# Layer 2 of two units of each pair by seven products summed in PSUM, with the groups ordered by a list scheduler

## The chip, the core and the metric

The kernel runs on one core of a Trainium2 chip. The metric is the device time of the whole program in microseconds (us), the median of three runs. Five engines work in parallel, each through its own queue in order: TensorE (PE in the profile, its weight loads PEld), VectorE (DVE), ScalarE (ACT), GpSimd (POOL) and SyncE (SP, which here only issues DMAs). PE writes to PSUM, which has eight banks of 128 x 512 fp32; the other operands lie in SBUF.

## The reference

A gated recurrence over 2 sequences of 6080 positions and 256 channels gives `h`, and a feed-forward layer with 2048 hidden columns follows:

```
f = lower_bound + (1 - lower_bound) * sigmoid(f_logit);  i = 1 - f
h[t] = f[t] * h[t-1] + i[t] * x[t]          # h starts at 0 in each sequence
a = h @ w_in                                # (12160, 256) @ (256, 2048), layer 1
g = a if a >= 1;  0 if a <= -1;  (a + 1)**2 / 4 between
out = g @ w_out                             # (12160, 2048) @ (2048, 256), layer 2
```

## The kernel before

The 12160 positions are cut into 24 tiles (all of 512 columns but one of 384). The hidden columns are cut into 8 units of 256 (`u`), each of two blocks of 128. Every product is done at nearly fp32 precision: each factor is split into a high and a low part (`xhi`/`xlo`, `ghi`/`glo`, `wi_hi`/`wi_lo`, `wo_hi`/`wo_lo`), and one product of a 128x128 weight block with 128x512 data is three matmuls (high*high, low*high, high*low). The low part of data costs one subtraction, the high part one cast.

**Stages.** The first four tiles, and all work on the weights, run in a first stage whose order is written out by hand (`ORDER`). From then on the 20 remaining tiles go in 10 pairs of neighbours (`pairs`), and each pair goes through the 8 units: 80 groups `g`, eight to a pair. In a group, layer 1 of a pair and a unit is a 2x2 block product (two column halves of the weight against two input halves of two tiles, eight block products), done by Strassen's scheme in Winograd's form with seven products `p1` to `p7` that are summed in PSUM (`pe1`, L988, with the table `SEVEN`, L981). The sums on the data side (`t1` to `t4`) are made in SBUF, and the intermediate sums by copies and additions between PSUM banks: `fork` (L999, ACT) copies bank Y into a new bank Q, `snap` (L994, ACT) copies Z to SBUF, `add_z` and `add_v` (L1004, L1007, DVE) add it to Y. At the end four banks Q, Z, V and Y hold the four blocks of `a`.

Each block then goes through a chain of five operations: `s_clip` (L1021, DVE, to [-1, 1]), `s_sq` (L1027, ACT, square of (c+1)/2), `s_max` (L1031, DVE, maximum with the bank, after which the bank is free), `s_hi_` (L1036, ACT, cast to `ghi`) and `s_lo_` (L1039, POOL, subtraction to `glo`).

**Layer 2** of a group (`fill_mm` and `triples`, L588) is eight products, each three matmuls, into four banks that belong to the pair (2 tiles x 2 output halves, `po`) for all its eight groups. They lag one group behind layer 1, and stand between its products. So a group is 7 + 8 = 15 products, 45 matmuls. At the end of a pair, `finish` (L654) copies the four banks out (three on ACT, one on DVE) and SP stores them. PSUM is full: four banks for the pair, four for the group, and a bank of the next group is one that the group before has given up.

**Order.** For the groups it is a table of times by hand: every operation has an offset from the group's start, `zt(g)` = 10.2 us times g (`at_time`, L956; `chain`, L1074), and all are emitted sorted by that time. The preparation of the next pair (`prepare`, L1125: loads, gate, recurrence `scan` on DVE, sums `t_sum` L915 and splits `f_hi`, `f_lo`) has places in the same table. Pools: three tiles of two blocks each for `g`, `ghi` and `glo` (`gp`, L213), two output tiles `o` (`op`).

Of the kernel before, what the change touches and what calls it, by code (L numbers as in the profile page):

```python
# [159 lines left out]

@with_exitstack
def gated_scan_then_ffn_kernel(
# [8 lines left out]

# [34 lines left out]
    KEPT = 5  # L206
    assert KD == 2 and KF == 16 and (len(tiles) - NC) % 2 == 0
# [5 lines left out]
    gp = ctx.enter_context(tc.tile_pool(name="gp", bufs=3))  # L213
# [305 lines left out]
    def plain_o(t, u, j, d):  # L519
        n = tiles[t][1]  # L520
        if (t, d) not in po:
            po[t, d] = bank()
        first = (t, d) not in started
        started.add((t, d))
        nc.tensor.matmul(  # L525
            out=po[t, d][:, :n], lhsT=vals[2 + 2 * u][:, j, d * P : (d + 1) * P], rhs=gg[t, u][:, j, :n],
            start=first, stop=False,
        )

    def clip(t, u, j):  # L530
        n = tiles[t][1]
        if (t, u) not in gg:
            gg[t, u] = gp.tile([P, 2, NMAX], F32, tag="g", name="g")
        nc.vector.tensor_scalar(
            out=gg[t, u][:, j, :n], in0=acc[t, u, j][:, :n], scalar1=-1.0, scalar2=1.0,
            op0=ALU.max, op1=ALU.min,
        )
# [3 lines left out]
    def clip_act(t, u, j):  # L541

        n = tiles[t][1]
        if (t, u) not in gg:
            gg[t, u] = gp.tile([P, 2, NMAX], F32, tag="g", name="g")
        c = gg[t, u][:, j, :n]
# [3 lines left out]
    def square(t, u, j):  # L550
        c = gg[t, u][:, j, : tiles[t][1]]
# [5 lines left out]
    def top(t, u, j):  # L557
        n = tiles[t][1]
        c = gg[t, u][:, j, :n]
# [8 lines left out]
    def g_hi(t, u, js=JA):  # L568
        n = tiles[t][1]
        if (t, u) not in ghi:  # L570
            ghi[t, u] = gp.tile([P, 2, NMAX], F32R, tag="ghi", name="ghi")
        s = slice(js[0], js[-1] + 1)
        nc.scalar.copy(out=ghi[t, u][:, s, :n], in_=gg[t, u][:, s, :n])

    def g_lo(t, u, js, eng):
        n = tiles[t][1]
        if (t, u) not in glo:
            glo[t, u] = gp.tile([P, 2, NMAX], F32R, tag="glo", name="glo")
        s = slice(js[0], js[-1] + 1)
        eng.tensor_tensor(  # L580
            out=glo[t, u][:, s, :n], in0=gg[t, u][:, s, :n], in1=ghi[t, u][:, s, :n],
            op=ALU.subtract,
        )

    def triple(t, d, u, i, a, b, first, last):
        triples(t, [d], u, i, a, b, first, last)

    def triples(t, ds, u, i, a, b, first, last, parts=range(3)):  # L588

        n = tiles[t][1]  # L590
        for q in parts:
            for d in ds:
# [5 lines left out]
                    start=not begun, stop=(last and q == 2),  # L598
                )

    def mm_o(t, u, js=JA, ds=range(KD), parts=range(3)):
        n = tiles[t][1]
        for j in js:
            for d in ds:
# [3 lines left out]
                t, ds, u, j, ghi[t, u][:, j, :n], glo[t, u][:, j, :n] if parts[-1] == 2 else None,  # L608
# [74 lines left out]
    with tc.manual_schedule():  # L683
# [156 lines left out]
        for kind, t, u, j in pe:  # L840
# [5 lines left out]
            if kind == "H":  # L846
# [20 lines left out]
                if "O" + i not in plain:  # L867
# [8 lines left out]
                    add("U" + i, "ACT", act(z), deps, g_hi, t, u, [j])  # L876
                    add("L" + i, "DVE|POOL", two(z), ["U" + i], on, g_lo, t, u, [j])
# [76 lines left out]
        ev = []  # L954

        def at_time(when, f, *args):  # L956
            ev.append((when, len(ev), f, args))

        TG = 10.2

        def zt(g):

            return g * TG

        def product(dst, p, u, wname, xname, start):
            if wname[0] == "a":
                i, k = int(wname[1]) - 1, int(wname[2]) - 1
                wh, wl = wi_hi[:, u, k, i], wi_lo[:, u, k, i]
            else:
                q = (int(wname[1]) - 1) * P  # L970
                wh, wl = (s[u // 2][:, u % 2, q : q + P] for s in (s_hi, s_lo))
            h, l = xhi[p, xname], xlo[p, xname]
            for q, (w, r) in enumerate([(wh, h), (wl, h), (wh, l)]):
                nc.tensor.matmul(  # L974
                    out=dst, lhsT=w, rhs=r, start=(start and q == 0), stop=(q == 2),
                    skip_group_check=True,
                )

        B = {}
        snaps = {}  # L980
        SEVEN = (  # L981
# [4 lines left out]
        )  # L986

        def pe1(g, name, role, w, x, start):  # L988
            p, u = divmod(g, NU)
            if (g, role) not in B:  # L990
                B[g, role] = bank()
            product(B[g, role], p, u, w, x, start)

        def snap(g):  # L994
            s = op.tile([P, NMAX], F32, tag="snap", name="snap", bufs=1)
            snaps[g] = s
            nc.scalar.copy(out=s, in_=B[g, "Z"])
# [3 lines left out]

# [9 lines left out]

        blocks = [("Q", 0, 0), ("Z", 1, 0), ("V", 1, 1), ("Y", 0, 1)]

        def gtile(d, g, b, dt, tag):
            if (g, b // 2) not in d:
# [226 lines left out]
```

## Time and profile before

| | |
|---|---|
| time, median of 3 runs (lowest, highest) | 1000.63 us (1000.56, 1000.72) |
| profiled execution, first to last instruction (span) | 999.2 us |
| median time less that span | 1.4 us |
| PE busy, of the span | 991.8 us, 99% |
| DVE, ACT, POOL busy | 741.7, 706.8, 639.7 us |
| first layer 1 product of the pairs starts | 173.5 us |
| granted TensorE clock, mean | 0.999 of full speed |

The profile is one execution of its own; of its time the trace gives the span, and the 1.4 us between it and the median of the timed runs lie outside the first and the last instruction. Busy time of PE counts a matmul from its start to the modelled end of its pipeline, so neighbours overlap: one lasts 0.39 us, but the next starts 0.23 us later.

### The profile page before, as it was taken

The page shows a single profiled execution, that of the slowest core. Times are in us where ns is not written, and L with a number is a line of the kernel's source. Part 1 is how long each engine was busy: PE and PEld are TensorE (multiplying, and loading weights), DVE is VectorE, ACT ScalarE, POOL GpSimd, SP SyncE. Part 2 cuts the span into 40 slices and gives each one's busy share as a digit, 9 for nine tenths or more (in the row PEclk, how much of TensorE's full clock was granted, in tenths as well). Part 3 has the DMA queues.
Part 4 walks back from the last instruction along what each step waited for, and adds up shares of the span by engine and source line. Part 5 has one row for each costly group of instructions (what it writes and reads, how often), then busy time and mean ns, then how long its engine had stood idle before and what let it go on. Part 6 is the DMA issues. An engine that isn't in the chain of part 4 may idle for free.

```text
span 999.2 us, 12745 instructions
## 1 busy us (share of the span) xinstructions
PE 991.8 (99%) x4374; PEld 816.2 (82%) x4374; DVE 741.7 (74%) x1129; ACT 706.8 (71%) x1230; POOL 639.7 (64%) x506
## 2 busy tenths in 40 slices
PE   8999999999999999999999999999999999999998
PEld 3888888888888888888888888888888888888886
DVE  8998998676677678677667668667767767776665
ACT  8988897766775775776676676677577667667555
POOL 1233326567767776876867777777687587777454
PEclk9999999999999999999999999999999999999999
DMA  9221020200200120030020020002002002001001
GB/s 346 85 69 59 22 100 1 85 21 1 106 22 1 48 80 1 0 106 22 1 106 22 0 106 22 1 26 97 5 1 105 22 1 85 1 1 43 0 1 43
DMA packets 17057, 46.56 MB, mean 47 GB/s; under 512 B 1888, under 2 KB 2912, under 8 KB 16992
## 3 DMA queue, kind: packets, MB, share of 16 engines
q1 hardware_dynamic: 16848, 45.62, 12.8%
q8 instruction: 34, 0.56, 0.2%
q14 instruction: 31, 0.25, 0.1%
q10 hardware_dynamic: 144, 0.13, 0.0%
HBM read 33.29 MB, written 12.45 MB: 46 GB/s over the span
## 4 chain that ended last, share of the span: by engine, by line
PE 98%; DVE 1%; DMA 0%; issue 0%; SPq 0%; DVEq 0%
PE bank L596 51%; PE bank L974 38%; PE bank L506 7%; PE bank L525 1%; DMA x<-in_fx 0%; PE bank L517 0%; DVE h L471 0%; DVE x L454 0%; DVE kept L339 0%; DVE kept L323 0%; DVE kept L344 0%; DVE g L562 0%; DVE kept L314 0%; DVE ea L274 0%; DVE o L630 0%
## 5 line engine op out<-in xcount | busy, mean ns | idle before, releaser
L1040 POOL TENSOR_TENSOR glo<-g,ghi 128x512 fp32r<-128x512 f32 x320 | 410.9, 1295 | 236.8 <-ACT ghi L1037 196.6
L1029 ACT ACTIVATE g<-g 128x512 f32<-128x512 f32 x320 | 200.8, 633 | 134.7 <-DVE g L1022 126.9
L1034 DVE TENSOR_TENSOR g<-g,bank 128x512 f32<-128x512 f32 x320 | 219.4, 686 | 80.0 <-ACT g L1029 65.3
L596 PE MATMUL bank<-ghi,wo_hi 128*128 128x512 f32 x759 | 259.0, 388 | 0.0
L596 PE MATMUL bank<-ghi,wo_lo 128*128 128x512 f32 x759 | 258.8, 387 | 0.0
L596 PE MATMUL bank<-glo,wo_hi 128*128 128x512 f32 x759 | 258.7, 387 | 0.0
L1037 ACT CAST ghi<-g 128x512 fp32r<-128x512 f32 x320 | 191.6, 626 | 70.3 <-DVE g L1034 68.5
L1022 DVE TENSOR_SCALAR g<-bank 128x512 f32<-128x512 f32 x320 | 213.8, 689 | 0.1
L596 PEld LDWEIGHTS bank<-ghi,wo_lo 128*128 128x128 f32 x759 | 142.2, 188 | 28.9 <-POOL wo_lo L353 0.3
L596 PEld LDWEIGHTS bank<-ghi,wo_hi 128*128 128x128 f32 x759 | 142.3, 188 | 28.8
L596 PEld LDWEIGHTS bank<-glo,wo_hi 128*128 128x128 f32 x759 | 142.3, 188 | 28.7
L1005 DVE TENSOR_TENSOR bank<-bank,snap 128x512 f32<-128x512 f32 x80 | 56.0, 700 | 111.5 <-ACT ghi L1037 109.4
L974 PE MATMUL bank<-xhi,s_hi 128*128 128x512 f32 x320 | 124.5, 389 | 0.0
L974 PE MATMUL bank<-xhi,s_lo 128*128 128x512 f32 x320 | 124.5, 389 | 0.0
L974 PE MATMUL bank<-xlo,s_hi 128*128 128x512 f32 x320 | 124.5, 389 | 0.0
L974 PE MATMUL bank<-xhi,wi_hi 128*128 128x512 f32 x240 | 93.4, 389 | 0.0
L974 PE MATMUL bank<-xhi,wi_lo 128*128 128x512 f32 x240 | 93.4, 389 | 0.0
L974 PE MATMUL bank<-xlo,wi_hi 128*128 128x512 f32 x240 | 93.4, 389 | 0.0
L1009 DVE TENSOR_TENSOR bank<-bank,snap 128x512 f32<-128x512 f32 x80 | 56.0, 700 | 43.5 <-PE bank L974 43.5
L1002 ACT COPY bank<-bank 128x512 f32<-128x512 f32 x80 | 45.6, 570 | 49.4 <-PE bank L974 49.4
L974 PEld LDWEIGHTS bank<-xlo,s_hi 128*128 128x128 f32 x320 | 60.1, 188 | 12.5
L974 PEld LDWEIGHTS bank<-xhi,s_lo 128*128 128x128 f32 x320 | 60.1, 188 | 12.5
(93 smaller groups left out, 1181.2 us busy)
## 6 DMA issues: line engine op xcount, KB each, us to landing
out_dram<-o SPq DMA_DIRECT2D x45, 256.0 KB, 2.1
f<-in_fx SPq DMA_DIRECT2D x22, 512.0 KB, 4.0
x<-in_fx SPq DMA_DIRECT2D x22, 512.0 KB, 4.3
raw<-in_w_out SPq DMA_DIRECT2D x8, 512.0 KB, 4.3
raw<-in_w_in SPq DMA_DIRECT2D x7, 512.0 KB, 5.6
raw<-in_w_in SPq DMA_DIRECT2D x2, 256.0 KB, 3.5
x<-in_fx SPq DMA_DIRECT2D x2, 256.0 KB, 4.1
f<-in_fx SPq DMA_DIRECT2D x2, 192.0 KB, 4.6
```

What stands on the lines that cost most here:

```text
L506: nc.tensor.matmul(out=acc[t, u, j][:, :n], lhsT=(wi_lo if q == 1 else wi_hi)[:, u, k, j], rhs=(xlo if q == 2 else xhi)[t, k][:, :n], star ...
L525: nc.tensor.matmul(out=po[t, d][:, :n], lhsT=vals[2 + 2 * u][:, j, d * P : (d + 1) * P], rhs=gg[t, u][:, j, :n], start=first, stop=False,)
L596: nc.tensor.matmul(out=po[t, d][:, :n], lhsT=w, rhs=b if q == 2 else a, start=not begun, stop=(last and q == 2),)
L974: nc.tensor.matmul(out=dst, lhsT=w, rhs=r, start=(start and q == 0), stop=(q == 2), skip_group_check=True,)
L1002: nc.scalar.copy(out=B[g, "Q"], in_=B[g, "Y"])
L1005: nc.vector.tensor_tensor(out=B[g, "Z"], in0=B[g, "Y"], in1=snaps[g], op=ALU.add)
L1009: nc.vector.tensor_tensor(out=B[g, "V"], in0=B[g, "Y"], in1=snaps[g], op=ALU.add)
L1022: nc.vector.tensor_scalar(out=gtile(gG, g, b, F32, "g"), in0=B[g, blocks[b][0]], scalar1=-1.0, scalar2=1.0, op0=ALU.max, op1=ALU.min,)
L1029: nc.scalar.activation(out=c, in_=c, func=AF.Square, bias=0.5, scale=0.5)
L1034: nc.vector.tensor_tensor(out=c, in0=c, in1=h, op=ALU.max)
L1037: nc.scalar.copy(out=gtile(hG, g, b, F32R, "ghi"), in_=gtile(gG, g, b, F32, "g"))
L1040: nc.gpsimd.tensor_tensor(out=gtile(lG, g, b, F32R, "glo"), in0=gtile(gG, g, b, F32, "g"), in1=gtile(hG, g, b, F32R, "ghi"), op=ALU.subtract,)
```

## The change

1. From the second pair on, units 0 and 1 of each pair (18 groups of 80) do layer 2 with the same seven-product scheme as layer 1. `pe2` issues the products (`CHAIN` names their operands). The two units are summed into the same four banks: each product is done for unit 0 and then for unit 1, and only then come the four steps between the banks, once for each pair: `fork2`, `snap2` (ACT), `add_z2`, `add_v2` (DVE). On the data side the four blocks of `g` need four sums `t1` to `t4` (`g_sum`), and seven splits in place of four (`chain_parts`). The weight sums `s1` to `s4` of the two units are made once, early in the groups, and are stored in blocks of `wi_hi` and `wi_lo` that are no longer read. All other units keep `item`, the eight products of before.
2. Layer 2 lags two groups (in the first eight groups the lag grows from one to two: `fills` gives them seven products of layer 2). In the third and fourth group of a pair the chain's products and one plain product stand (the rows `A`).
3. The table of times is gone. `Steady` is a list scheduler: jobs have a kind (engine, occupancy and latency by `OCC`), dependencies, buffers and banks that they use, and PE's order is given; jobs of the other engines are taken by their due times. Sums and splits marked `either` go to POOL, or to DVE when they are urgent. Two-input SBUF work of DVE and POOL's work share one resource, `port`, in the scheduler; in the emitted program nothing orders them.
4. For 130 of the 320 blocks (`RELU`) the clip moves from DVE to ACT (`s_relu`), as the first stage does it already.
5. Pools: single blocks, 14 for `g` and 6 each for `ghi` and `glo`; the outputs of both tiles and `snap2` share the two tiles `o`. The first stage keeps its order.

```diff
+class Steady:
+    OCC = {
+        "copy": ("ACT", 0.485, 0.59, False), "act": ("ACT", 0.525, 0.63, False), "gate": ("ACT", 0.96, 1.06, False),
+        "forget": ("ACT", 0.625, 0.73, False), "psum": ("DVE", 0.605, 0.695, False), "sbuf": ("DVE", 0.605, 0.695, True),
+        "scan": ("DVE", 1.22, 1.31, True), "small": ("DVE", 0.205, 0.3, True), "pool": ("POOL", 1.24, 1.30, True),
+        "either": ("POOL", 1.24, 1.30, True), "load": ("SP", 0.6, 5.0, False),
+    }
...
+            if e != "PE" and (e == "POOL" or self.OCC[kind][3]):
+                s = max(s, port)
...
-    gp = ctx.enter_context(tc.tile_pool(name="gp", bufs=3))
+    gp = ctx.enter_context(tc.tile_pool(name="gp", bufs=6))
...
+        def s_relu(g, r):
+            gG[g, r] = gp.tile([P, NMAX], F32, tag="g", name="g", bufs=GB)
+            nc.scalar.activation(out=gG[g, r], in_=B[g, r], func=AF.Relu, bias=0.5, scale=0.5)
...
+        def g_sum(g, to, x, y, eng):
+            eng.tensor_tensor(out=gG[g, to], in0=gG[g, x], in1=gG[g, y], op=ALU.subtract)
...
+        CHAIN = {
+            "p5": ("Z", "s1", "t1"), "p1": ("Y", "a11", "Q"), "p6": ("Y", "s2", "t2"), "p2": ("Q", "a12", "Y"),
+            "p7": ("Y", "s3", "t3"), "p3": ("Z", "s4", "V"), "p4": ("Y", "a22", "t4"),
+        }
...
+        def fork2(p):
+            k = out_of(p, "Q")
+            po[k] = bank()
+            started.add(k)
+            nc.scalar.copy(out=po[k], in_=po[out_of(p, "Y")])
...
+        RELU = ["QZ", "Y", "Y", "QVY", "Z", "Y", "QVY", "Z"]
...
+            parts(g, "Q", "Q", [m("Q")])
+            total(1, "Q", "Z", "Q", [l("Q"), m("Z")])
+            parts(g, "Q", "t1", [f"t1_{g}"])
+            total(2, "Q", "V", "Q", [l("t1"), m("V")])
+            parts(g, "Q", "t2", [f"t2_{g}"])
+            total(3, "Z", "V", "Z", [f"t1_{g}", m("V")])
+            parts(g, "Z", "t3", [f"t3_{g}"])
+            parts(g, "V", "V", [m("V")])
+            parts(g, "Y", "Y", [m("Y")])
+            total(4, "Y", "Y", "Q", [l("Y"), f"t2_{g}"])
+            parts(g, "Y", "t4", [f"t4_{g}"])
...
+        A = ["p1 p1", "p5 p5 p2", "p2 p6", ""], ["p6 x", "p7 p7 p3", "p3 p4", "p4"]
```

The first place is PE in the third group of the fourth pair (g = 26), from layer 1's `p1` to its `p6`; a row is one matmul, with the tile it writes, its data and its weights. Before:

```order
L974 MATMUL bank_4058<-xhi_3462,wi_hi_84 128x512
L974 MATMUL bank_4058<-xhi_3462,wi_lo_85 128x512
L974 MATMUL bank_4058<-xlo_3481,wi_hi_84 128x512
L596 MATMUL bank_3972<-ghi_4023,wo_hi_86 128x512
L596 MATMUL bank_3973<-ghi_4023,wo_hi_86 128x512
L596 MATMUL bank_3972<-ghi_4023,wo_lo_87 128x512
L596 MATMUL bank_3973<-ghi_4023,wo_lo_87 128x512
L596 MATMUL bank_3972<-glo_4030,wo_hi_86 128x512
L596 MATMUL bank_3973<-glo_4030,wo_hi_86 128x512
L974 MATMUL bank_4058<-xhi_3716,s_hi_1496 128x512
```

And now:

```order
L1103 MATMUL bank_4340<-xhi_3970,wi_hi_84 128x512
L1103 MATMUL bank_4340<-xhi_3970,wi_lo_85 128x512
L1103 MATMUL bank_4340<-xlo_4065,wi_hi_84 128x512
L1103 MATMUL bank_4348<-ghi_4262,wo_hi_86 128x512
L1103 MATMUL bank_4348<-ghi_4262,wo_lo_87 128x512
L1103 MATMUL bank_4348<-glo_4268,wo_hi_86 128x512
L1103 MATMUL bank_4348<-ghi_4298,wo_hi_86 128x512
L1103 MATMUL bank_4348<-ghi_4298,wo_lo_87 128x512
L1103 MATMUL bank_4348<-glo_4309,wo_hi_86 128x512
L1103 MATMUL bank_4340<-xhi_4067,s_hi_1572 128x512
```

Before, the two products between `p1` and `p6` share one block of `g` and write two banks; now they are the chain's first product for unit 0 and for unit 1, on two blocks of `g` (of g = 24 and of g = 25) into one bank.

The second place is ACT at the same point, around the copy `fork` of g = 26 (L1002 before, L1126 now; L1029, L1149 and L1151 are squares, L1037 and L1163 casts to `ghi`, L445 the gate's `forget`, L798 copies an output out, L1145 is `s_relu`, L1254 `fork2`). The brackets name the engines that a row waits for. Before:

```order
L1029 ACTIVATE g<-g 128x512 [waits DVE_49]
L1029 ACTIVATE g<-g 128x512 [waits DVE_49,Activation_49]
L1037 CAST ghi<-g 128x512 [waits DVE_49]
L1029 ACTIVATE g<-g 128x512 [waits DVE_49]
L1002 COPY bank<-bank 128x512 [waits DVE_49,PE_49]
L997 COPY snap<-bank 128x512 [waits Activation_49]
```

And now:

```order
L1151 ACTIVATE g<-g 128x512 [waits DVE_49] x2
L1163 CAST ghi<-g 128x512
L1145 ACTIVATE g<-bank 128x512 [waits PE_49]
L798 COPY o<-bank 128x512
L1163 CAST ghi<-g 128x512 [waits DVE_49,Activation_49]
L1126 COPY bank<-bank 128x512 [waits PE_49]
L1149 ACTIVATE g<-g 128x512 [waits Activation_49]
L798 COPY o<-bank 128x512 [waits DMAHW1_49]
L1122 COPY snap<-bank 128x512
L1254 COPY bank<-bank 128x512 [waits PE_49,Activation_49]
```

Directly ahead of `fork` now stands the cast of the sum `t1` of g = 25, which waits for DVE; before, a square stood there.

The third place is DVE just ahead of that (L1022 and L1139 clip, L1034 and L1159 maximum, L1005 and L1129 `add_z`, L471 the recurrence, L1170 the sum `t1` of g = 25, L1167 its low part). Before:

```order
L1022 TENSOR_SCALAR g<-bank 128x512 [waits DVE_49,Pool_49]
L1034 TENSOR_TENSOR g<-g,bank 128x512 [waits Activation_49]
L1022 TENSOR_SCALAR g<-bank 128x512 [waits PE_49]
L1034 TENSOR_TENSOR g<-g,bank 128x512 [waits Activation_49] x2
L471 SCALAR_TENSOR_TENSOR h<-f,h,x 128x64 [waits DMAHW2_49,Pool_49]
L471 SCALAR_TENSOR_TENSOR h<-f,x 128x448
L1005 TENSOR_TENSOR bank<-bank,snap 128x512 [waits PE_49,Activation_49]
```

And now:

```order
L1139 TENSOR_SCALAR g<-bank 128x512 [waits PE_49]
L1139 TENSOR_SCALAR g<-bank 128x512 [waits DVE_49]
L1159 TENSOR_TENSOR g<-g,bank 128x512 [waits Activation_49] x2
L1170 TENSOR_TENSOR g<-g 128x512 [waits DVE_49,Pool_49]
L1167 TENSOR_TENSOR glo<-g,ghi 128x512 [waits PE_49,Activation_49]
L1154 SCALAR_TENSOR_TENSOR g<-bank,g 128x512 [waits Activation_49]
L1129 TENSOR_TENSOR bank<-bank,snap 128x512 [waits PE_49,Activation_49]
```

A sum and a subtraction with both inputs in SBUF now stand on DVE between the maxima and `add_z`, work that was POOL's alone in the groups before, or was not there.

## Rows read from the trace of the kernel before

**Rows 1.** The page's busy times and its chain that ended last.

```profile
span 999.2 us, 12745 instructions
...
PE 991.8 (99%) x4374; PEld 816.2 (82%) x4374; DVE 741.7 (74%) x1129; ACT 706.8 (71%) x1230; POOL 639.7 (64%) x506
...
PE 98%; DVE 1%; DMA 0%; issue 0%; SPq 0%; DVEq 0%
```

**Rows 2.** Windows: stage and its length, busy us by engine, clock, DMA.

```profile
0.00:20.00 20.00, 16.41 (x46) 6.65 (x47) 15.03 (x33) 16.66 (x33) 3.54 (x8) 1.00 0.92 346
...
100.00:172.00 72.00, 72.00 (x332) 61.20 (x331) 68.53 (x118) 60.40 (x111) 27.54 (x21) 1.00 0.13 43
...
580.00:662.00 82.00, 82.00 (x364) 67.89 (x363) 58.82 (x86) 56.69 (x97) 60.32 (x49) 1.00 0.11 39
...
990.00:999.20 9.20, 5.34 (x27) 4.35 (x25) 2.65 (x5) 3.49 (x6) 3.85 (x3) 0.90 0.31 115
```

**Rows 3.** One line's instructions: `fork`, its count, durations (ns), first and last start.

```profile
L1002 ACT COPY bank<-bank x80: 570/570/590, 175.3 to 981.1; 128x512 f32<-128x512 f32 x80
```

**Rows 4.** Timeline, one group: start, duration, engine, instruction [idle before <-releaser].

```profile
603.24 0.39 PE L974 MATMUL bank<-xlo,wi_hi 128*128 128x512 f32 x1
...
603.62 1.28 DVE L471 TENSOR_TENSOR_SCAN h<-f,h,x 128x512 f32<-128x512 f32 x1
603.67 0.57 ACT L1002 COPY bank<-bank 128x512 f32<-128x512 f32 x1 [0.68 <-PE bank L974]
...
604.63 1.15 ACT L1037 CAST ghi<-g 128x512 fp32r<-128x512 f32 x2
...
605.39 2.55 POOL L1040 TENSOR_TENSOR glo<-g,ghi 128x512 fp32r<-128x512 f32 x2 [1.70 <-ACT ghi L1037]
...
609.79 1.29 DVE L1022 TENSOR_SCALAR g<-bank 128x512 f32<-128x512 f32 x2
```

**Rows 5.** Groups of instructions by line and shape: busy us, mean ns | idle before.

```profile
L1040 POOL TENSOR_TENSOR glo<-g,ghi 128x512 fp32r<-128x512 f32 x320 | 410.9, 1295 | 236.8 <-ACT ghi L1037 196.6 <-issue 21.4 <-POOL xlo L483 10.1
...
L1022 DVE TENSOR_SCALAR g<-bank 128x512 f32<-128x512 f32 x320 | 213.8, 689 | 0.1
L1029 ACT ACTIVATE g<-g 128x512 f32<-128x512 f32 x320 | 200.8, 633 | 134.7 <-DVE g L1022 126.9 <-ACT f L432 3.7 <-issue 1.4
L1037 ACT CAST ghi<-g 128x512 fp32r<-128x512 f32 x320 | 191.6, 626 | 70.3 <-DVE g L1034 68.5
...
L1005 DVE TENSOR_TENSOR bank<-bank,snap 128x512 f32<-128x512 f32 x80 | 56.0, 700 | 111.5 <-ACT ghi L1037 109.4 <-PE bank L974 2.0
...
L997 ACT COPY snap<-bank 128x512 f32<-128x512 f32 x80 | 47.5, 593 | 0.0
...
L547 ACT ACTIVATE g<-bank 128x512 f32<-128x512 f32 x48 | 28.5, 594 | 8.4 <-PE bank L506 7.6 <-PE bank L517 0.5
...
L580 DVE TENSOR_TENSOR glo<-g,ghi 128x512 fp32r<-128x512 f32 x26 | 18.4, 718 | 1.3 <-ACT ghi L573 1.3
```

**Rows 6.** Waits: who waited for whom, us in total, times, longest.

```profile
DVE bank L1005 <- ACT ghi L1037: 109.4, 78, 2.1
ACT bank L1002 <- PE bank L974: 49.4, 79, 0.7
```

**Rows 7.** Timeline of DVE and of POOL in the first stage, and L363's durations.

```profile
153.95 1.29 DVE L363 TENSOR_TENSOR whole<-wi_hi,wi_lo 128x512 f32<-128x512 f32 x1
...
159.73 1.79 DVE L363 TENSOR_TENSOR whole<-wi_hi,wi_lo 128x512 f32<-128x512 f32 x1
...
153.39 1.30 POOL L483 TENSOR_TENSOR xlo<-x,xhi 128x512 fp32r<-128x512 f32 x1 [0.30 <-DVE bank L375]
...
159.16 1.80 POOL L580 TENSOR_TENSOR glo<-g,ghi 128x512 fp32r<-128x512 f32 x1 [0.20 <-POOL x L915]
...
L363 DVE TENSOR_TENSOR whole<-wi_hi,wi_lo x8: 684/686/1789, 130.1 to 166.6; 128x512 f32<-128x512 f32 x8
```

**Rows 8.** The page's DMA issues: count, KB each, median us to landing.

```profile
out_dram<-o SPq DMA_DIRECT2D x45, 256.0 KB, 2.1
```

More of the change, by code (lines that the diff above doesn't have):

```diff
@@ L550, in square @@
     def square(t, u, j):
[L551 removed]
+        c = gg[t, u, j][:, : tiles[t][1]]
         if (t, u, j) in clipped:
@@ L597, in triples @@
                     out=po[t, d][:, :n], lhsT=w, rhs=b if q == 2 else a,
-                    start=not begun, stop=(last and q == 2),
+                    start=not begun, stop=(last and q == 2), skip_group_check=(t >= NC),
                 )
@@ L875, in gated_scan_then_ffn_kernel @@
                         ]
-                    add("U" + i, "ACT", act(z), deps, g_hi, t, u, [j])
-                    add("L" + i, "DVE|POOL", two(z), ["U" + i], on, g_lo, t, u, [j])
+                    add("U" + i, "ACT", act(z), deps, g_hi, t, u, j)
+                    add("L" + i, "DVE|POOL", two(z), ["U" + i], on, g_lo, t, u, j)
             else:
@@ new lines, in gated_scan_then_ffn_kernel, with three, pe1 @@
+        blocks = [("Q", 0, 0), ("Z", 1, 0), ("V", 1, 1), ("Y", 0, 1)]
+        home2 = {"Q": (0, 0), "Z": (1, 0), "V": (1, 1), "Y": (0, 1)}
+        B, snaps = {}, {}
+        def three(dst, wh, wl, h, l, start):
+            for q, (w, r) in enumerate([(wh, h), (wl, h), (wh, l)]):
+                nc.tensor.matmul(
+                    out=dst, lhsT=w, rhs=r, start=(start and q == 0), stop=(q == 2), skip_group_check=True,
+                )
+        def pe1(g, name):
+            p, u = divmod(g, NU)
+            role, w, x, start = SEVEN[name]
+            if (g, role) not in B:
+                B[g, role] = bank()
+            if w[0] == "a":
+                i, k = int(w[1]) - 1, int(w[2]) - 1
@@ L979, in gated_scan_then_ffn_kernel @@
-        B = {}
-        snaps = {}
-        SEVEN = (
[4 rows of a table removed]
[L986 to L992, printed above, removed]
+            three(B[g, role], wh, wl, xhi[p, x], xlo[p, x], start)
         def snap(g):
-            s = op.tile([P, NMAX], F32, tag="snap", name="snap", bufs=1)
-            snaps[g] = s
-            nc.scalar.copy(out=s, in_=B[g, "Z"])
+            snaps[g] = op.tile([P, NMAX], F32, tag="snap", name="snap", bufs=1)
@@ L999, in fork @@
+            nc.scalar.copy(out=snaps[g], in_=B[g, "Z"])
         def fork(g):
@@ new lines, in out_of, with pe2 @@
+        def out_of(p, r):
+            side, d = home2[r]
+            return pairs[p][side], d
+        def pe2(p, u, name):
+            r, w, x = CHAIN[name]
+            k = out_of(p, r)
+            begun = k in started
+            started.add(k)
+            if k not in po:
+                po[k] = bank()
+            if w[0] == "a":
+                d, i = int(w[1]) - 1, int(w[2]) - 1
+                wh, wl = (s[:, u, i, d * P : (d + 1) * P] for s in (wo_hi, wo_lo))
+            else:
+                q = 4 * CH.index(u) + int(w[1]) - 1
+                wh, wl = wi_hi[:, q, 0, 1], wi_lo[:, q, 0, 1]
+            g = p * NU + u
+            three(po[k], wh, wl, hG[g, x], lG[g, x], not begun)
@@ new lines, in gated_scan_then_ffn_kernel, with snap2, add_z2 @@
+        snap2s = {}
+        def fork2(p):
+            k = out_of(p, "Q")
+            po[k] = bank()
+            started.add(k)
+            nc.scalar.copy(out=po[k], in_=po[out_of(p, "Y")])
+        def snap2(p):
+            snap2s[p] = op.tile([P, NMAX], F32, tag="o", name="snap2")
+            nc.scalar.copy(out=snap2s[p], in_=po[out_of(p, "Z")])
+        def add_z2(p):
+            z = po[out_of(p, "Z")]
+            nc.vector.tensor_tensor(out=z, in0=po[out_of(p, "Y")], in1=snap2s[p], op=ALU.add)
```

639 lines of the change are left out of this document (458 added, 181 removed), and 4 rows, old and new, of the table SEVEN.

## The prediction

> **What bounds the kernel now.** I read the page's busy times first, then the chain that ended last [rows 1]. PE is busy for 99% of the span, 98% of the chain lies on it, and no other engine is above 74%. The windows by stage say where [rows 2]: PE is busy for all 82.00 us of a stretch in the groups and all 72.00 us of one in the first stage. Only the ends have idle time, 3.6 us in the first 20 and 3.9 us in the last 9.2.
>
> Busy time alone does not give the price of a matmul, since neighbours overlap. The pace does: the copy `fork` comes once a group, and the first and the last of its 80 starts are 805.8 us apart, 79 groups [rows 3], so a group lasts 10.20 us. With 45 matmuls that is 0.2267 us each, 0.68 us for a product. Priced at the 0.39 us that one row shows [rows 4], a removed matmul would seem worth too much, 21 us in all for the 54 below. (The Trainium skill, "Trainium Kernel Development and Optimization", Best Practices, warns of the same: matmul busy time is no measure of the distance to the peak.)
>
> **What is removed.** In 18 groups (two units of nine pairs) layer 2 takes seven products instead of eight: 18 x 3 = 54 matmuls, 54 x 0.2267 = 12.24 us. PE waits for nothing in the groups, so all of it is on the path. Without any new wait the time is 1000.63 - 12.24 = 988.4 us; against the profiled execution, whose span is 999.2 us with 1.4 us around it, a span of 987.0 us. Removing a wait cannot add to this, because there is none in the groups; the first stage keeps its order, and the end still has its last products, copies and stores. For shifts at the two ends I allow 0.4 us, which makes the lower bound 988.0 us.
>
> **What is added, by engine.** PE's freedom now rests on the others.
> - ACT: 54 more casts (7 splits for 4 in 18 groups) at 0.626, 130 clips moved from DVE at 0.594 (the first stage's clips on ACT), and 18 copies between the pair's banks at some 0.59 [rows 5]: 33.8 + 77.2 + 10.6 = 121.6 us, 1.5 us a group. A pair had 56.7 us of ACT in about 82 [rows 2], and now has some 69 in 80.2, 86%.
> - DVE: 130 clips leave (130 x 0.689 = 89.6 us); 65 subtractions, 19 of the new sums and 17 more splits of the next pair's data come, 101 x 0.718, and 18 additions between banks at 0.700 [rows 5], 85.1 us. No change in load, 73%.
> - POOL: 53 sums come, 11 + 17 splits go and a few weight operations come, some 29 x 1.295 = 38 us [rows 5], from 74% to about 80%.
>
> So no engine becomes the bound by load. These loads take each operation at its full length; behind each other they follow faster, two casts in 1.15 us and two clips in 1.29 us [rows 4]. The weight sums of the two units and SP's stores have slack of whole groups. Two output tiles instead of four: the copy `snap2` needs the tile whose store was issued some 2.4 us earlier, and a store lands in 2.1 us [rows 8], so it is covered by about 0.3 us, and would delay ACT's queue behind it by what is missing.
>
> **Where PE can come to wait.** I walked the order through the third group of the fourth pair, time 0 being the start of `p5` of g = 26, a product every 0.68 us. The first possible wait is `p6`, which needs `fork`. Between `p5` and `p6` stand `p1` and the chain's first two products, so `p6` starts at 2.72. `fork` reads what `p1` wrote: `p1` starts at 0.68, its last matmul at 1.13, and a copy starts 0.43 us behind that start [rows 4], at 1.56, and ends at 2.13. The slack is 0.6 us, if ACT is free.
>
> But ahead of `fork` on ACT stands the cast of the sum t1 of g = 25, and this sum is now on DVE, with both inputs in SBUF. When can it start? `p3` of g = 25 starts at -3.40, DVE reads its bank at -2.51, then come two clips, two squares on ACT, two maxima: the sum at about 0.1. Just there POOL gets its next subtraction: the cast before it ends at about -0.03, and POOL starts 0.13 us behind a cast [rows 4], at 0.1. It is a tie, and it matters who is first. What happens when both want SBUF stands in the first stage [rows 7]: a DVE addition of two SBUF tiles that takes 0.68 alone took 1.29 when a POOL subtraction had started 0.56 us before it, and ended 0.55 us after POOL's end; another took 1.79, 1.11 more. If DVE is first, its sum ends at 0.8, the cast at 1.5, and `fork` is on time. If POOL is first, the sum ends at 0.1 + 1.30 + 0.55 = 1.95, the cast at 2.6, `fork` runs from 2.55 to 3.12, and `p6` waits 0.4 us, with the signal to PE about 0.5. The fourth to ninth pair have this sequence: 6 x 0.5 = 3.0 us as one bound, 0 as the other. I take the middle, 1.5 us. (The Trainium skill, "SBUF — State Buffer", Who interferes with whom, puts it as a rule: a VectorE instruction with two SBUF inputs and a GpSimd instruction that reads SBUF exclude each other for a whole instruction, and who issues first wins. The trace agrees; by it the longest block is one POOL operation, 1.30 us.)
>
> Besides this one a pair has nine more such DVE operations. Each can be held up by 0 to 1.11 us, but those that I followed have over 1.5 us until PE needs their result (the low part of this t1 is wanted at 5.2, that of Y at 7.9). I put 0.1 us a pair on them, 0.9 us in all.
>
> The sum: 1000.63 - 12.24 + 1.5 + 0.9 = **990.8 us**, faster by 1.0%.
>
> **The rivals.**
> 1. Everything is hidden. DVE wins the tie, or ACT makes it up: 988.4 us (988.0 to 989.5). For it: even the tightest slack is 0.4 us, and the hand-timed kernel lost nothing with waits of DVE and ACT of similar tightness (`fork` waits for PE in 79 of 80 groups, by 0.7 us at most [rows 6]). Against it: fixed queues with more work on each.
> 2. The short groups are too short. 26 groups now have 14 products instead of 15 (the first eight, and the third and fifth of nine pairs), 9.52 us. The next group's `p1` takes the bank that Z gives up: in g = 26 `p3` starts at 6.8, then clip, square and maximum in series end at 9.8 [rows 4, 5], and `p1` starts at 10.2. That is 0.4 us of slack where 15 products leave 1.1. One DVE operation of 0.6 us in front of one of the three costs 0.2 us, a blocked one more, 0.6: 26 x 0.2 to 0.6 is 5.2 to 15.6 us, at 0.3 each 996.2 us. For it: ACT's load in the short groups comes near their length. Against it: the scheduler sorts by due time, and my walk found none in front.
> 3. Slower, by the shared port. The hand-written table kept POOL idle around DVE's two-input work: a scan on DVE runs from 603.62 to 604.90 while POOL is idle for 1.70 us [rows 4]. The new program has no such order. A pair has ten two-input operations on DVE beside its four scans; each that reaches PE costs 0.5 to 1.11 us. The saving of a pair is 1.36 us, so from two of ten on it is gone. With three at 0.75 us the time is 988.4 + 9 x 2.25 = 1008.6 us.
> 4. It does not do what it says: the matmuls do not fall, or PE waits for the longer data chain (two splits and a sum in series). The order shows 54 matmuls fewer, so only the second is left, and the low part of t1 of g = 24 has some 4 us to spare; about 1000 us.
>
> **How the numbers follow.** The forecast (989.5 to 992.5) has 0.40, rival 1 0.25, rival 2 0.23 (992.5 to 1000, 0.15 of it below 996.5), rival 3 0.08, rival 4 0.04. The range 988.0 to 996.5 us holds 0.40 + 0.25 + 0.15 = 0.80. A change within 0.2% (2 us) is about what a measurement of this kernel cannot tell from none. Faster by more: 0.40 + 0.25 + 0.21 = 0.86; the same: 0.02 + 0.04 = 0.06; slower: 0.08.
>
> **What would show it right or wrong.** In the profile after, the matmuls are 4320 and still follow at 0.2267 us in the plain groups. A pair should last 80.2 us plus its waits; the waits of PE should name ACT's copy `fork` in the third group of the fourth to ninth pair, 0.4 to 0.6 us each, and the DVE sum in front of it should last about 1.9 us instead of 0.7. If these sums last 0.7, rival 1 holds; if PE waits for DVE's maxima at `p1` of the groups after short ones, rival 2; if many DVE rows of two SBUF inputs last over 1.2 us and PE waits for their results, rival 3. The forecast is wrong if PE's waits in the groups add up to more than 4 us or to less than 1.

## The result, and the profile after

| | before | changed |
|---|---|---|
| time, median (lowest to highest) | 1000.64 us (1000.56 to 1000.72) | 1012.15 us (1011.88 to 1015.91) |
| ratio, 95% interval | | 1.0121 (1.0105 to 1.0137) |
| span of the profiled execution | 999.2 us | 1010.1 us |

The change makes the kernel slower by 1.2%, where 1.0% faster was forecast. The page of the changed kernel against [rows 1]: the matmuls fell by 54 as counted, PE's share fell to 98%, and DVE and POOL are each busier than the loads in the prediction allow: DVE 788.4 us where "no change" was expected, POOL 713.8 us where 38 us on 639.7 were. The chain that ended last, which lay on PE for 98%, now leaves it for 23% of the span, about half of that to DVE.

```profile
span 1010.1 us, 12953 instructions
...
PE 990.7 (98%) x4320; PEld 803.9 (80%) x4320; DVE 788.4 (78%) x1126; ACT 786.5 (78%) x1434; POOL 713.8 (71%) x535
...
PE 77%; DVE 11%; issue 4%; ACT 4%; POOL 2%; DMA 0%; SPq 0%; DVEq 0%; ACTq 0%; POOLq 0%
```

The same stretch as in [rows 2] (window and length, busy us and instructions by engine, clock, DMA): PE did 352 matmuls in 82 us instead of 364.

```profile
580.00:662.00 82.00, 80.48 (x352) 65.35 (x351) 65.52 (x87) 63.90 (x117) 65.69 (x48) 1.00 0.12 39
```

Where the added busy time sits is seen in the instructions of single lines (count, then shortest, median and longest duration in ns, first and last start): the sums of the new scheme (L1170) on DVE, their splits (L1167) on DVE, and the scans (L622).

```profile
L1170 DVE TENSOR_TENSOR g<-g x19: 677/1776/1799, 279.1 to 947.7; 128x512 f32<-128x512 f32 x19
...
L1167 DVE TENSOR_TENSOR glo<-g,ghi x65: 658/684/1840, 256.6 to 951.2; 128x512 fp32r<-128x512 f32 x65
...
L622 DVE TENSOR_TENSOR_SCAN h<-f,h,x x44: 558/1615/2380, 31.0 to 901.9; 128x512 f32<-128x512 f32 x42, 128x64 f32<-128x64 f32 x2
```

A sum takes 0.68 us alone, and 1.78 us in the median. Now the place that the prediction walked through, the third group of the fourth pair: DVE, POOL, ACT and PE in the timeline of the changed kernel (start, duration, engine, line, what; in brackets the idle time before and what ended it).

```profile
436.56 1.29 DVE L1159 TENSOR_TENSOR g<-g,bank 128x512 f32<-128x512 f32 x2
437.77 1.79 DVE L1170 TENSOR_TENSOR g<-g 128x512 f32<-128x512 f32 x1
...
437.72 1.29 POOL L1167 TENSOR_TENSOR glo<-g,ghi 128x512 fp32r<-128x512 f32 x1 [0.17 <-ACT ghi L1163]
438.97 1.75 POOL L1170 TENSOR_TENSOR g<-g 128x512 f32<-128x512 f32 x1
...
439.65 0.62 ACT L1163 CAST ghi<-g 128x512 fp32r<-128x512 f32 x1 [1.04 <-DVE g L1170]
440.17 0.59 ACT L1126 COPY bank<-bank 128x512 f32<-128x512 f32 x1
...
440.19 0.39 PE L1103 MATMUL bank<-glo,wo_hi 128*128 128x512 f32 x1
440.81 0.50 PE L1103 MATMUL bank<-xhi,s_hi 128*128 128x512 f32 x1 [0.24 <-ACT bank L1126]
441.15 0.39 PE L1103 MATMUL bank<-xhi,s_lo 128*128 128x512 f32 x1
```

POOL's subtraction starts at 437.72, DVE's sum 0.05 us later at 437.77, and the sum ends at 439.56, 0.55 us after POOL's end at 439.01: the picture of [rows 7]. The cast waits 1.04 us for it, `fork` comes behind the cast, and `p6` starts 0.62 us after the matmul before it instead of 0.227; the next one is also 0.11 us late. That is 0.51 us. It comes in the fourth to the tenth pair, seven times, with POOL 0.050 to 0.055 us ahead each time.

A second place costs more, 6.6 us in all: `p4` in the first group of a pair (here the fifth, g = 32), which needs `add_v` (L1133) on DVE:

```profile
504.73 1.78 DVE L1167 TENSOR_TENSOR glo<-g,ghi 128x512 fp32r<-128x512 f32 x1
506.43 1.77 DVE L634 TENSOR_TENSOR xlo<-x,xhi 128x512 fp32r<-128x512 f32 x1
508.12 0.69 DVE L1133 TENSOR_TENSOR bank<-bank,snap 128x512 f32<-128x512 f32 x1
...
504.13 3.52 POOL L1167 TENSOR_TENSOR glo<-g,ghi 128x512 fp32r<-128x512 f32 x2
...
507.83 0.39 PE L737 MATMUL bank<-glo,wo_hi 128*128 128x512 f32 x1
508.96 0.47 PE L1103 MATMUL bank<-xhi,wi_hi 128*128 128x512 f32 x1 [0.74 <-DVE bank L1133]
```

Two splits, 0.68 us each alone, follow each other on DVE while POOL has two of its own; the four take turns, the splits last 1.78 and 1.77 us, and POOL's pair 3.52 instead of 2.55. `add_v`, which stands behind them in DVE's queue, ends 2.2 us later than it would, and PE waits 1.0 us (1.6 us in the third pair; the fourth and the eighth pair have no such wait). In the fourth group of a pair the same happens with a split and a sum ahead of `add_z` (L1129):

```profile
450.63 1.46 DVE L1167 TENSOR_TENSOR glo<-g,ghi 128x512 fp32r<-128x512 f32 x1
452.01 1.77 DVE L1170 TENSOR_TENSOR g<-g 128x512 f32<-128x512 f32 x1
453.71 0.68 DVE L1129 TENSOR_TENSOR bank<-bank,snap 128x512 f32<-128x512 f32 x1
...
454.45 0.50 PE L1103 MATMUL bank<-xhi,s_hi 128*128 128x512 f32 x1 [0.37 <-DVE bank L1129]
```

Here `p7` and the chain's first `p4` wait, 1.05 us together, in six of the seven pairs from the fourth on; in the seventh pair POOL does not get in front of the sum, which lasts 0.68 us, and PE does not wait.

Summed over the whole trace (each start of a matmul in the groups against 0.2267 us after the one before, differences from 0.03 us up), PE waits 20.9 us: 1000.64 - 12.24 + 20.9 = 1009.3 us. The other 2.8 us are not in these waits. The first pair starts 0.5 us later than before, differences below 0.03 us add 1.5 us more than before, and 0.5 us more lie outside the span (1012.0 us for the profiled execution, with a span of 1010.1).

### The profile page after: what moved, and what is told of

It is laid out like the page before. It is cut to its first block, busy times and chain, and to the rows that moved or that the text cites. A ratio compares the mean times of both kernels' runs of the same rounds, so it can differ in the third digit from the quotient of the medians.

```text
span 1010.1 us, 12953 instructions
## 1 busy us (share of the span) xinstructions
PE 990.7 (98%) x4320; PEld 803.9 (80%) x4320; DVE 788.4 (78%) x1126; ACT 786.5 (78%) x1434; POOL 713.8 (71%) x535
## 4 chain that ended last, share of the span: by engine, by line
PE 77%; DVE 11%; issue 4%; ACT 4%; POOL 2%; DMA 0%; SPq 0%; DVEq 0%; ACTq 0%; POOLq 0%
PE bank L1103 35%; PE bank L737 34%; PE bank L657 7%; DVE g L1170 2%; DVE xlo L634 2%; POOL glo L1167 2%; ACT ghi L1163 1%; DVE glo L1167 1%; DVE g L1139 1%; DVE g L1159 1%; DVE bank L1133 1%; ACT g L1145 1%; ACT g L1151 1%; PE bank L676 1%; DVE bank L1129 1%
## 5 line engine op out<-in xcount | busy, mean ns | idle before, releaser
L1167 POOL TENSOR_TENSOR glo<-g,ghi 128x512 fp32r<-128x512 f32 x309 | 425.1, 1388 | 147.7 <-ACT ghi L1163 104.6
L1163 ACT CAST ghi<-g 128x512 fp32r<-128x512 f32 x374 | 224.0, 615 | 32.8 <-PE bank L1103 14.4
L737 PE MATMUL bank<-ghi,wo_hi 128*128 128x512 f32 (+1 forms) x615 | 228.9, 387 | 0.0
L737 PE MATMUL bank<-glo,wo_hi 128*128 128x512 f32 (+1 forms) x615 | 228.7, 387 | 0.0
L737 PE MATMUL bank<-ghi,wo_lo 128*128 128x512 f32 (+1 forms) x615 | 228.6, 387 | 0.0
L1151 ACT ACTIVATE g<-g 128x512 f32<-128x512 f32 x190 | 118.6, 631 | 80.3 <-DVE g L1139 79.2
L1159 DVE TENSOR_TENSOR g<-g,bank 128x512 f32<-128x512 f32 x190 | 128.0, 684 | 56.1 <-ACT g L1151 51.5
L1139 DVE TENSOR_SCALAR g<-bank 128x512 f32<-128x512 f32 x190 | 128.1, 686 | 1.7
L1154 DVE SCALAR_TENSOR_TENSOR g<-bank,g 128x512 f32<-128x512 f32 x130 | 89.1, 685 | 43.0 <-ACT g L1149 42.3
L1145 ACT ACTIVATE g<-bank 128x512 f32<-128x512 f32 x130 | 77.1, 595 | 52.9 <-PE bank L1103 37.4
L1129 DVE TENSOR_TENSOR bank<-bank,snap 128x512 f32<-128x512 f32 x80 | 55.6, 695 | 47.1 <-PE bank L1103 21.7
L1149 ACT ACTIVATE g<-g 128x512 f32<-128x512 f32 x130 | 82.0, 631 | 1.5
L1170 POOL TENSOR_TENSOR g<-g 128x512 f32<-128x512 f32 x53 | 76.3, 1442 | 6.0 <-DVE glo L1167 4.4
```

The lines of the kernel that those rows point to most:

```text
L737: nc.tensor.matmul(out=po[t, d][:, :n], lhsT=w, rhs=b if q == 2 else a, start=not begun, stop=(last and q == 2), skip_group_check=(t >= NC),)
L1139: nc.vector.tensor_scalar(out=gG[g, r], in0=B[g, r], scalar1=-1.0, scalar2=1.0, op0=ALU.max, op1=ALU.min,)
L1145: nc.scalar.activation(out=gG[g, r], in_=B[g, r], func=AF.Relu, bias=0.5, scale=0.5)
L1149: nc.scalar.activation(out=gG[g, r], in_=gG[g, r], func=AF.Square)
L1151: nc.scalar.activation(out=gG[g, r], in_=gG[g, r], func=AF.Square, bias=0.5, scale=0.5)
L1154: nc.vector.scalar_tensor_tensor(out=gG[g, r], in0=B[g, r], scalar=1.0, in1=gG[g, r], op0=ALU.max, op1=ALU.min)
```

## The experiments

**The scheduler's own order, enforced.** The scheduler counts DVE's two-input work and POOL's work as one resource, but the program holds nothing to it. Here it is held in both directions.

```diff
+        held = None
+        for f, e, port in st.run(begin, done):   # port: POOL's jobs, DVE's sums, splits, scans
             f(e)
+            if port:
+                made = tc.nc.cur_bb.bb.instructions[-1]
+                if held is not None and held[0] != e:
+                    tc.add_manual_dep(made, held[1].name, ...)
+                held = e, made
```

> The changed kernel with nothing taken away; added are waits that hold DVE's operations of two SBUF inputs (sums, splits, scans) and POOL's operations, in the groups, to the one order that the scheduler gave them, so that no two of them overlap. Theory (port): PE's 20.9 us of waits come from POOL starting ahead of, or into, a DVE operation that the scheduler had put first; with the order kept, DVE's sum ahead of fork lasts 0.7 instead of 1.78 us, PE's waits fall below 4 us, and the time to 988.4 + 0 to 4 = 988.5 to 992.5 us. Rival (load and queues): ACT, DVE and POOL have too much in line in the third and fourth group of a pair whatever the overlap; added waits then only cost, and the time stays at 1012 us or above. Rival (short groups): waits move to p1 behind 14-product groups, about 996 us.

Measured: 1000.75 us, 0.9992 of before (0.9982 to 1.0002). DVE's sums last 0.69 us, and PE's waits fall from 20.9 to 10.2 us, so the overlap is a cause, and load alone is not. But 10 us remain, and DVE itself now waits, 68 us in these four rows (who waited for whom: us in total, times, longest; lines are one further than in the changed kernel, as in most kernels below).

```profile
DVE xlo L635 <- POOL glo L1168: 23.2, 7, 3.4
DVE h L623 <- POOL glo L1168: 19.7, 18, 1.6
DVE glo L1168 <- POOL glo L1168: 18.9, 17, 1.5
...
DVE glo L1168 <- POOL g L1171: 6.3, 17, 0.6
```

**Only POOL waits.** The same with one condition more.

```diff
-                if held is not None and held[0] != e:
+                if held is not None and held[0] != e and e == "POOL":
```

> As the kernel with the full order, but only POOL waits: a POOL operation waits for the last DVE operation of two SBUF inputs that the scheduler put ahead of it; DVE never waits for POOL. Theory (port): what hurts is POOL cutting in ahead of DVE by some tens of ns, with DVE's queue, ACT's cast and PE behind it, so this half does most of the work: 989 to 995 us, DVE's sums at 0.7 us. If as much comes from DVE arriving in the middle of a POOL operation that the scheduler had put ahead of it, that remains and the time is between, 995 to 1008 us. Rival (load and queues): 1012 us or above.

Measured: 991.67 us, 0.9902 of before (0.9887 to 0.9917). This is the forecast's number, from the changed program with nothing but waits of POOL added. The place of above in its timeline: DVE's sum takes 0.69 us, POOL's subtraction starts 0.16 us behind its end, and `fork` (L1127) starts at 433.61, when `p1` is ready, with no wait of PE at `p6` (434.77).

```profile
432.12 0.69 DVE L1171 TENSOR_TENSOR g<-g 128x512 f32<-128x512 f32 x1
...
432.97 1.29 POOL L1168 TENSOR_TENSOR glo<-g,ghi 128x512 fp32r<-128x512 f32 x1 [1.08 <-ACT o L799]
...
432.89 0.62 ACT L1164 CAST ghi<-g 128x512 fp32r<-128x512 f32 x1
433.61 0.57 ACT L1127 COPY bank<-bank 128x512 f32<-128x512 f32 x1
...
434.54 0.39 PE L1104 MATMUL bank<-glo,wo_hi 128*128 128x512 f32 x1
434.77 0.39 PE L1104 MATMUL bank<-xhi,s_hi 128*128 128x512 f32 x1
```

PE is again busy for the whole of a stretch, with 363 matmuls in 82 us, and its waits in the groups sum to 1.75 us. POOL's own start can still be ahead of DVE's: the scans (L623 here) still take 1.56 us in the median, where one took 1.28 us in [rows 4], and PE does not wait for that.

```profile
580.00:662.00 82.00, 82.00 (x363) 67.85 (x362) 65.31 (x91) 66.63 (x120) 62.76 (x50) 1.00 0.11 36
...
L623 DVE TENSOR_TENSOR_SCAN h<-f,h,x x44: 622/1562/2379, 29.9 to 883.1; 128x512 f32<-128x512 f32 x42, 128x64 f32<-128x64 f32 x2
```

**Only DVE waits**, the other half (`e == "DVE"` in the condition).

> The changed kernel with the other half of the order alone: a DVE operation of two SBUF inputs waits for the last POOL operation that the scheduler put ahead of it; POOL never waits for DVE, so it can still start first. Theory (direction: what hurts is POOL ahead of DVE, and holding DVE for POOL only adds to it): no gain, 1010 to 1020 us, with DVE's sums still at 1.8 us where POOL starts just ahead. Rival (any kept order helps; the full order lost to the half only because of the number of waits): 1000 us or less.

Measured: 1026.08 us, 1.0258 of before (1.0237 to 1.0279), slower still than expected and 1.4% above the changed kernel. PE's waits in the trace sum to 39.3 us, and the 0.51 us behind `fork` is still there in all seven pairs. So the direction decides: POOL ahead of DVE costs, and DVE held for POOL costs more. The likely reason, which no run tests by itself: DVE's queue holds `add_z`, `add_v`, clips and maxima, which PE needs within a group, and POOL's queue holds mostly low parts that PE needs a group or more later.

**Which of DVE's operations matter.** POOL waits for sums only, for splits only, for scans only.

```diff
-        port = lambda n, e: e == "POOL" or (e == "DVE" and jobs[n][0] in ("either", "scan", "small"))
+        port = lambda n, e: e == "POOL" or (e == "DVE" and (n[0] == "t" or n[:2] == "xt"))   # sums
+        port = lambda n, e: e == "POOL" or (e == "DVE" and (n[:2] in ("lo", "xl")))          # splits
+        port = lambda n, e: e == "POOL" or (e == "DVE" and (n[:4] == "scan"))                # scans
```

> The changed kernel, POOL waiting only for DVE's sums (t1 to t4, 19 in all), not for its splits and scans. Theory (port): the sum ahead of the cast and of fork then lasts 0.7 us, so p6 of the third group of a pair no longer waits (7 x 0.51 us), and p7 of the fourth waits less (6 x 0.64 us); add_v of the first group of a pair stands behind splits and stays late (7 x 1.0 us). From the changed kernel 5 to 8 us are gained: 1004 to 1007 us, 1.003 to 1.006 of before, with p4 of the first group still waiting 0.9 us. Rival (any few waits shift the queues and mend all): near 0.990.

Measured: 1000.98 us, 0.9997 (0.9982 to 1.0012), the median of ten runs that spread from 997.5 to 1004.9 us.

> The changed kernel, POOL waiting only for DVE's splits (low parts of layer 2's data and of the next pair, 82 in all), not for its sums and scans. Theory (port): p4 of the first group of a pair no longer waits for add_v (7 x 1.0 us), p7 of the fourth group waits less; p6 of the third group still waits 0.5 us for fork behind the sum on DVE. 8 to 12 us are gained: 1000 to 1004 us, 0.999 to 1.003 of before. Rival (the sums carry most of it): above 1.006.

Measured: 995.5 us, 0.9940 (0.9926 to 0.9955).

> The changed kernel, POOL waiting only for DVE's scans (38), not for its sums and splits. Theory (port): the scans stand in groups where DVE has slack, so that what they are held up by reaches PE in one or two places only; 0 to 3 us are gained, 1009 to 1012 us, 1.008 to 1.012 of before. Rival (the scans are the long operations and carry the loss): below 1.004.

Measured: 1016.89 us, 1.0159 (1.0133 to 1.0185).

PE's waits in the four traces, and in the one where POOL waits for all three, by place, in us (start to start, as above):

| place of PE's wait | changed | sums | splits | scans | all three |
|---|---|---|---|---|---|
| `p6` of the third group, behind `fork` | 3.6 | 0 | 3.6 | 3.6 | 0 |
| `p7` and the chain's `p4` of the fourth group, six pairs from the fourth on | 6.3 | 0 | 0 | 6.2 | 0 |
| `p4` of the first group, behind `add_v` | 6.6 | 6.7 | 0 | 10.7 | 0 |
| elsewhere, mostly the first three pairs | 4.4 | 5.9 | 1.8 | 3.8 | 1.75 |
| sum | 20.9 | 12.6 | 5.4 | 24.3 | 1.75 |

Each of the three places goes with its own operations. The 0.51 us behind `fork` vanishes when POOL waits for sums and stands unchanged, in all seven pairs, when it waits for splits; the wait behind `add_v` does the opposite. In the fourth group either is enough. Scans carry none of the three: held for scans, POOL loses time (in the kernel with all three it waits 32 us for them) and the first group gets worse. Both the sums and the splits gained more than expected, mainly because each mends the fourth group alone, which the expectations shared out between them. By the spans of these traces (999.9 and 992.8 against 1010.1 us) they gained 1.9 and 1.8 us more than the table shows; which differences below 0.03 us make that up was not followed. The same is read from the rows of PE's waits (us in total, times, longest; they count only the time in which PE had nothing under way, so they are smaller than the table). Where POOL waits for splits only, PE waits for `fork` (L1127 there):

```profile
PE bank L1104 <- ACT bank L1127: 1.7, 7, 0.3
```

Where it waits for sums only, PE waits for `add_v` (L1134 there):

```profile
PE bank L1104 <- DVE bank L1134: 5.5, 7, 1.4
```

Seven times each: for `fork` once in each pair from the fourth on, for `add_v` twice in the third pair (its first and its fourth group) and once in the first group of the fifth, sixth, seventh, ninth and tenth.

**Sums and splits without scans, and the best once more.** The condition takes the kind `either` alone.

> The changed kernel, POOL waiting for DVE's sums and splits, not for its scans. Waiting for scans alone cost 4 us, for sums alone gained 11 us, for splits alone 17 us. Theory (each wait pays where DVE's queue is needed by PE soon, and scans are not): 989.5 to 992 us, as good as with all three or up to 1.5 us better. Rival (the scans' waits are needed with the others to keep the order together): 993 to 997 us.

Measured: 991.79 us, 0.9909 (0.9893 to 0.9926).

> The kernel in which POOL waits for all of DVE's two-input operations once more, beside the two others on one chip: 0.989 to 0.992 of before.

Measured: 991.56 us, 0.9906 (0.9891 to 0.9921). On one chip the two cannot be told apart: the waits for scans cost nothing once the others are there, and bring nothing. The best kernel is the changed one with POOL held behind DVE, 0.990 of before, twice.

**Everything on POOL.** No sum or split goes to DVE.

```diff
-URGENT = 3.0
+URGENT = -1000.0
```

> The changed kernel with every sum and split on POOL (the scheduler's urgency bound set so that none goes to DVE); on DVE only the scans still have two SBUF inputs. Theory (port): no sum on DVE is held up any more, p6 of the third group no longer waits for fork behind it, and add_v of the first group of a pair comes in time; but POOL has 106 more operations of 1.3 us, some 15 us a pair, and in the chain's groups comes late: PE waits for POOL's low parts instead, so the total can be 1000 to 1030 us. Rival (load and queues): the same waits for fork, add_z and add_v stay, with the DVE operations at 0.69 us.

Measured: 1025.5 us in one run, beside 1001.46 us before. Of the waits for `fork`, `add_z` and `add_v`, only 0.37 us in the third pair are left in the groups of the chain. PE waits 35.9 us in all. Some 30 us of it are waits for POOL's low parts; another 4.8 us are three stretches of 3.4 to 3.5 us behind such waits, in the eighth to tenth pair, in which the granted clock was 0.52 to 0.53 and the matmuls followed each other at 0.43 us. POOL has 101 operations more than the changed kernel (636 for 535), not the 106 of the expectation. So without DVE's share of this work POOL comes late.

**The order without the seven products.** All units take eight products, with the new scheduler, lag, pools and clips.

```diff
-        CH = (0, 1)
+        CH = ()
-            if p and u in (2, 3):
+            if CH and p and u in (2, 3):
-            q = p if u >= (1 if p == 0 else 4) else p - 1
-            k = 7 if (q == 0 and g < NU + 1) or (q and u == 4) else 8
+            q = p if u >= (1 if p == 0 else 2) else p - 1
+            k = 7 if q == 0 and g < NU + 1 else 8
```

> The changed kernel without the seven products of layer 2: all units take the eight products, with the lag of two groups, the scheduler, the moved clips and the new pools as they are; 54 matmuls more than the changed kernel, as many as before. The scheduler then puts two sums or splits on DVE in the whole program, instead of 101. Theory (port): the waits come with DVE's two-input operations, of which only the scans are left; 1000.6 us and up to 4 us of waits, 1000.5 to 1004.5 us. Rival (the scheduler's order itself, or the deeper lag, loses against the hand-written table): 1008 us or more, 8 us above the kernel before with the same matmuls.

Measured: 1008.86 us, 1.0074 (1.0053 to 1.0095), beyond what was expected of the overlap: the rival's bound was met. In the trace, which is of the slowest of its four runs (1006.4 to 1011.1 us), PE's waits are 9.4 us, and half of them hang on one operation, a split on DVE early in the second pair:

```profile
255.86 5.56 DVE L1167 TENSOR_TENSOR glo<-g,ghi 128x512 fp32r<-128x512 f32 x1
...
255.85 1.31 POOL L634 TENSOR_TENSOR xlo<-h,xhi 128x512 fp32r<-128x512 f32 x1
257.10 1.31 POOL L634 TENSOR_TENSOR xlo<-x,xhi 128x512 fp32r<-128x512 f32 x1
258.34 2.52 POOL L1167 TENSOR_TENSOR glo<-g,ghi 128x512 fp32r<-128x512 f32 x2
```

The two windows behind it (window and length, busy us and instructions of PE, PEld, DVE, ACT and POOL, then clock, DMA share and GB/s):

```profile
258.00:261.50 3.50, 1.14 (x6) 0.60 (x5) 3.50 (x2) 1.23 (x2) 2.87 (x3) 1.00 0.74 241
261.50:266.00 4.50, 4.50 (x12) 3.29 (x13) 3.70 (x6) 1.43 (x3) 1.28 (x1) 0.62 0.00 0
```

The split is passed by four POOL operations in a row and ends 0.56 us after the last; PE waits 2.5 us for it. In the 4.5 us after that the granted clock is 0.62 in the mean, so for most of them it was at 1.2 of its two levels, 1.2 and 2.4 GHz: 12 matmuls were done, where the pace of 0.2267 us gives 20, which is 1.8 us more. The wait alone does not decide this: where POOL waits for sums only, PE waits 2.6 us at the same place, behind a split of 5.59 us, and the clock stays at 1.00 in the same stretch.

```profile
258.00:261.50 3.50, 1.07 (x5) 0.61 (x4) 3.50 (x2) 1.23 (x2) 2.61 (x3) 1.00 0.64 211
261.50:266.00 4.50, 4.39 (x19) 3.31 (x19) 3.45 (x6) 2.76 (x6) 1.30 (x1) 1.00 0.01 2
```

The two theories part with POOL held back in this kernel too:

> The kernel without layer 2's seven products (54 more matmuls than the changed one, as many as before), with POOL held behind DVE's two-input operations as in the kernel that came to 0.990 of before. It tells what the scheduler's order costs by itself. Without the waits it was 1.0074 of before. Theory (port, now through the scans and one split): its 9.4 us of PE waits come from scans of up to 2.3 us and one split of 5.6 us on DVE; held back, POOL lets them run in 1.3 and 0.7 us, PE's waits fall below 1.5 us, the time to 0.999 to 1.002 of before. Rival (the order itself loses): it stays at 1.006 or more.

Measured: 1002.22 us, 1.0009 (0.9999 to 1.0019), and 0.3 us of waits in the groups. The order itself loses 0.2% at most; the rest of its loss was the overlap as well. Against it the seven products bring 0.9906 / 1.0009 = 0.990, and 54 matmuls at 0.2267 us are 1.2%, of which PE's waits of 1.75 us against 0.3 take 0.15%.

## Why the prediction was wrong

**The saving was right.** 54 matmuls went, the pace in free stretches is 0.2267 us as before, and where PE does not wait, as in the kernel with POOL held back, the time is 991.67 us beside 1001.46 us of the kernel before: 1001.46 - 12.24 + 1.75 is 991.0.

**The place was right, the tie was not a tie.** For `p6` behind `fork` the walk put DVE's sum and POOL's subtraction both at 0.1 us behind the start of `p5`; in the trace POOL is 0.05 us ahead, in each of seven pairs. The wait was put at 0.4 to 0.5 us and is 0.51 us. What failed is the halving: the same order comes back in each of these pairs, so this race had no mean. At its bound the term was 7 x 0.51 = 3.6 us instead of 1.5 (the prediction counted six pairs, the tenth has it too).

**The step that failed is the 0.1 us a pair for the nine other operations.** In its place stand 20.9 - 3.6 = 17.3 us of waits instead of 0.9: 6.3 in the fourth groups, 6.6 in the first groups and 4.4 elsewhere in the first three pairs. All but 1.75 us go when POOL is held behind DVE. The reason given, over 1.5 us until PE needs their result, looked at the wrong thing. PE waited for such a result itself only once, 0.4 us in the second pair. What was late is what stood behind them in DVE's queue: `add_v` behind two splits, `add_z` behind a split and a sum. Two such operations in a row were also held up twice, 2.2 us in all, where the sum assumed one block of at most 1.11 us. The walk had gone through `fork`'s queue on ACT in this way, but not through DVE's own in the first and the fourth group.

**The rivals.** Rival 3, slower by the overlap of DVE's two-input operations with POOL, is what happened, and it had a chance of 0.08. Its threshold (1.36 us a pair) was passed in every pair from the fourth on, with 2.5 us in four of the seven and 1.5 to 1.6 us in the other three; its 1008.6 us stand against 1012.15. Its remark that the new program has no order between the two was the whole point: the scheduler puts the two in turn, the program lets them meet. Rival 2 did not come: PE's waits at `p1` of the group after a short one are one of 0.44 us in the seventh group of the first pair. Rival 4 did not come either. One more point: by the rule of the Trainium skill, "SBUF — State Buffer", Who interferes with whom, the prediction took one POOL operation as the longest block. The runs disagree: the changed kernel has a DVE split of 4.85 us and the kernel without the seven products one of 5.56, so a single DVE operation can lose against several of POOL in a row, and the measurement decides.

**The loads.** ACT's 786.5 us are less than 706.8 + 121.6, since operations behind each other overlap in part. DVE's "no change" missed some 47 us and POOL's 38 us became 74. With POOL held back they are 763.7 and 674.8 us, so 25 of DVE's 47 us and 39 of POOL's 74 were time of being blocked, counted as busy. The other 22 us of DVE were not taken apart; the scans, still at 1.56 us there, are part of them.

```profile
PE 981.3 (99%) x4320; PEld 805.9 (81%) x4320; DVE 763.7 (77%) x1126; ACT 791.5 (80%) x1434; POOL 674.8 (68%) x535
```

## What to carry to other kernels

A scheduler that reckons with a shared resource should also write its order into the program, as waits, where two queues meet there. Here that paid only in the direction in which POOL waits: the other direction cost more than no order. When an operation gets slower, look at what stands behind it in its own queue before looking at who reads its result. A race of 0.05 us between two queues fell the same way in all seven rounds here, so price such a race at its bound, times the rounds. Not every race did: the waits behind `add_v` skip two pairs, and four runs of the changed kernel spread over 4.0 us where four of the kernel with POOL held back spread over 1.2.

## What the runs showed of the hardware that was not expected

A DVE operation of two SBUF inputs that meets POOL usually waited for one POOL operation and then ran (1.78 us), with the next POOL operation held up in turn (1.75 us in place of 1.30). But in five traces (the changed kernel, the one without the seven products, and those with waits for sums only, for scans only and of DVE only) eleven operations lasted 3.0 to 5.6 us. All eleven are splits (with everything on POOL, one scan took 3.54 us). In the changed kernel the one at 337.79 took 4.85 us, and in the kernel without the seven products one took 5.56 us, for an operation of 0.68: each ended 0.55 us after the fourth POOL operation in a row, and each of those four lasted 1.28 to 1.33 us. In the six traces in which POOL waits for splits there is none. What decides between one POOL operation and several was not tried and stays open.

The clock is open too. After PE's wait of 2.5 us the granted clock was 0.62 in the next 4.5 us; after one of 2.6 us at the same place in another kernel it was 1.00. With everything on POOL the fourth to the tenth pair have almost the same waits, up to 1.6 us each, and the clock was at its lower level behind them in the eighth to tenth only. In the stretch of the changed kernel from 580 to 662 us, with waits of up to 1 us, it stayed at 1.00.
